# Attention softmax shared between ScalarE and VectorE: VectorE's exponential rebuilt as a sum of four shifted bit patterns, PSUM banks shared, order model remeasured

## The chip, the cores and the metric

The kernel runs on one core of a Trainium2 chip. The metric is the device time of one execution in microseconds (us). Five engines matter: TensorE (PE, with its weight loads PEld), VectorE (DVE), ScalarE (ACT), GpSimd (POOL) and SyncE (SP, which here only issues transfers). TensorE's clock is granted by a throttle, and the trace records it: 1.00 is full speed, 0.50 is half.

On one core a run counts as *slow* when it is more than 1.5% above the fastest run of the same kernel.

## The reference, cut to what matters

```python
# x: [1, 2048, 640], bf16; 32 heads of 20 for the queries, ONE head of keys and values
def reference(...):
    xn = layernorm(x)
    return x + A(xn) + B(xn)

def A(x):                                   # attention, all heads share k and v
    q = (x @ wq) -> [heads, 2048, 20];  k = x @ wk;  v = x @ wv
    p = softmax(q k^T * 20**-0.5)           # 32 x 2048 x 2048 exponentials
    return (p v) @ wo

def B(x):                                   # feed-forward, inner width 1536
    return relu(x @ w1 + b1)**2 @ w2 + b2
```

Most of the time goes to the 134 million exponentials of the softmax.

## The kernel before

The scores are cut into 2,048 tiles of 128 keys x 512 queries: 32 blocks (8 groups of four heads x 4 query chunks), 16 key tiles each, 4 heads each. Per tile, TensorE computes K x Q into one PSUM bank, an engine computes exp from PSUM into SBUF, and TensorE multiplies the result with V. "QK" is the first product and "PV" the second. Four heads run side by side on TensorE: QK tiles the array by rows (contraction over 20 values), and PV and everything else tiles it by columns.

Two engines make exponentials. ScalarE does it directly, on three banks or on two at a time, in alternation:

```python
ACT_BANKS = ((0, 1, 2), (3, 4))     # ScalarE's two sides: 3 banks, then 2
DBANKS = (5,)                       # VectorE's one bank
PVB = 6                             # PV sums
MB = 7                              # projections, FFN, output, one at a time
...
Op(f"ACT{j}", "ACT", 0.064 + 0.4267 * n, [activation(out=PT[:, s0:s0+n, :], in_=ps[:, b0:b0+n, :], func=Exp, ...)])
```

VectorE does it in *sets* of four tiles (four heads of one key tile), by writing an integer into the bit pattern of a bf16 number. `L = x*XA + XB` as a 16-bit integer, read as bf16, is a power of two with a linear mantissa. That is a rough exp. The kernel corrects it with two more terms, made from the same bits:

```python
# four evictions from PSUM, one per tile
d1 = tensor_scalar(out=L[:, cs] as uint16, in0=ps[:, bank, :], scalar1=XA, scalar2=XB, mult, add)      # 0.686
# once per set, on 128 x 2048
W  = tensor_scalar(L, 0xFF80, 124,    bitwise_and, bitwise_or)      # 0.74, the power of two
U  = tensor_scalar(L, 0x7F,   0x3F80, bitwise_and, bitwise_or)      # 0.74, the mantissa
T  = tensor_tensor(L, U, mult)                                      # 1.235
T  = tensor_tensor(T, U, mult)      # VectorE 1.235, in every second set GpSimd in two halves of 2.15
# TensorE adds up: L @ vx  +  W @ (0.5*vx)  +  T @ (CC*vx)           three weighted sums per set
```

The order of all instructions is fixed when the program is built. A greedy list scheduler in Python gives every operation a modelled duration (the numbers in the margins) and a modelled latency between engines. At each step it takes the operation that can start first. VectorE takes a set whenever it has room, and ScalarE gets the other tiles. So *the model decides how many tiles each engine gets*. Where the model sees TensorE less than `FILL` busy during a wait, the scheduler inserts *fillers*: matmuls with zero weights into the PV bank that change nothing and only keep TensorE running:

```python
FILL = 0.7
...
lat = 0.2 if the producer is PE else 0.06                  # latency model
...
while pick[0] > free["PE"] + 0.1 + ... and pe_credit(free["PE"]) < 0.0:      # modelled PE use below FILL
    commit(Op("fill", "PE", 0.215, [mm(ps[...PVB...], zeros32, kT[:, 0:512], False, False, ...) for jj in range(4)]))
```

The softmax here doesn't subtract the row's maximum and nothing guards it: scores larger than these inputs give would overflow.

## Time and profile before

Three runs: 837.78, 837.86 and 1253.41 us. Nothing was recorded that explains the third.

| before, one profiled execution | value |
|---|---|
| span | 840.8 us, mean granted clock 0.962 |
| first exponential starts / last ends | 31.8 / 831.9 us |
| tiles on ScalarE / VectorE | 1,696 / 352 (88 sets) |
| exponential activations | 679 (339 of three banks, 339 of two, 1 rest) |
| filler groups of four matmuls | 272 |

The first fence is cut from the page of the kernel before. It shows the engines' busy times, two rows of busy tenths (40 equal slices of 21 us; PEclk is the granted clock in tenths), the chain that ended last by engine, and then groups of instructions. A group's line gives the source line, engine, operation, output<-input with shapes and count, then busy us and the mean ns of one, then the engine's idle time just before these instructions and what ended it.

```profile
PE 775.6 (92%) x10439; PEld 254.9 (30%) x10439; DVE 678.5 (81%) x973; ACT 794.5 (94%) x724; POOL 268.4 (32%) x168
...
ACT  7589999997989999999999999999899999999995
...
PEclk8689999987989999999999999999999999999999
...
ACT 61%; PE 28%; DVE 6%; issue 1%; DVEq 0%
...
L862 ACT ACTIVATE PT<-ps 128x1536 bf16<-128x1536 f32 (+1 forms) x679 | 775.0, 1294 | 29.3 <-PE ps L549 27.5
...
L978 DVE TENSOR_SCALAR x_sb<-ps 128x512 uint16<-128x512 f32 x352 | 241.3, 685 | 113.2 <-PE ps L549 110.7
...
L989 DVE TENSOR_TENSOR tbuf<-x_sb,ubuf 128x2048 bf16<-128x2048 bf16 x88 | 113.4, 1289 | 0.6
...
L549 PE MATMUL ps<-kT,zeros 128*32 128x512 bf16 x1088 | 87.9, 401 | 0.0
...
L985 DVE TENSOR_SCALAR x_sb<-x_sb 128x2048 uint16<-128x2048 uint16 x88 | 68.6, 780 | 0.5
L987 DVE TENSOR_SCALAR ubuf<-x_sb 128x2048 uint16<-128x2048 uint16 x88 | 66.4, 755 | 0.0
L996 DVE TENSOR_TENSOR tbuf<-tbuf,ubuf 128x2048 bf16<-128x2048 bf16 x44 | 55.5, 1261 | 0.0
```

ScalarE is the bound: 775.0 us of exponentials, and only 29.3 us idle before them, of which 4.3 come before the first one. VectorE's four set operations (the last four DVE lines) cost 304 us against 241 us for the evictions. The line with `kT,zeros` is the fillers: 272 groups of four.

The PEclk row has two dents, at the start and around slices 8 to 11, counted from zero. This is the window view of the kernel before for the second dent. Its columns are window, us, then the busy us of PE, PEld, DVE, ACT and POOL with their counts, granted clock, DMA share and GB/s.

```profile
180.00:200.00 20.00, 19.04 (x150) 4.35 (x153) 11.01 (x18) 14.67 (x13) 5.68 (x3) 0.58 0.01 2
```

With the clock at 0.58, ScalarE was busy only 14.67 of 20 us although TensorE was busy 19.04. It waits there for a TensorE at half speed.

### The profile page before, as it was taken

The numbers are of one execution on the slowest core, as the hardware profiler recorded it, in microseconds if no ns is written. First come the engines' busy times: TensorE is split into PE (matmuls) and PEld (weight loads), VectorE is DVE, ScalarE is ACT, GpSimd is POOL, SyncE is SP. The second block draws the span as 40 slices with busy tenths as digits, with TensorE's granted clock in tenths as the row PEclk, the third lists the DMA queues.
The fourth block names the chain that finished last, engine by engine and source line by source line (L and its number), as shares of the span: only waits on it lengthen the run. The fifth ranks groups of instructions, "written<-read, shape, count | busy, mean of one in ns | idle before, by whom it ended". The sixth has DMA issues, their size and how long they took to land.

```text
span 840.8 us, 22953 instructions
## 1 busy us (share of the span) xinstructions
PE 775.6 (92%) x10439; PEld 254.9 (30%) x10439; DVE 678.5 (81%) x973; ACT 794.5 (94%) x724; POOL 268.4 (32%) x168
## 2 busy tenths in 40 slices
PE   7799999999999999899999999999899999999996
PEld 3232222222223333222223333322222333323332
DVE  5768888776878888889887877889888888888874
ACT  7589999997989999999999999999899999999995
POOL 4424344531222321254432223135343232223221
PEclk8689999987989999999999999999999999999999
DMA  9500000000000000000000000000000000000000
GB/s 306 120 2 2 1 2 2 2 2 1 2 2 17 3 17 18 17 2 2 2 2 2 17 18 17 3 16 2 2 2 2 18 17 18 17 2 2 3 2 33
DMA packets 11714, 14.94 MB, mean 18 GB/s; under 512 B 2017, under 2 KB 10978, under 8 KB 11618
## 3 DMA queue, kind: packets, MB, share of 16 engines
q1 hardware_dynamic: 10306, 13.44, 5.2%
q8 instruction: 81, 1.33, 0.7%
q10 hardware_dynamic: 1312, 0.05, 0.1%
q14 instruction: 15, 0.12, 0.0%
HBM read 10.87 MB, written 2.62 MB: 16 GB/s over the span
## 4 chain that ended last, share of the span: by engine, by line
ACT 61%; PE 28%; DVE 6%; issue 1%; DVEq 0%
ACT PT L862 61%; PE ps L549 28%; DVE x_sb L978 2%; DVE tbuf L989 1%; DVE T L914 1%; DVE ubuf L987 1%; DVE x_sb L985 0%; DVE hT_tmp L668 0%; PE ps L597 0%; DVE out_sb L1171 0%; DVE Tn L912 0%; DVE qT L651 0%; DVE kT L611 0%; DVE OTn L918 0%; PE ps L624 0%
## 5 line engine op out<-in xcount | busy, mean ns | idle before, releaser
L862 ACT ACTIVATE PT<-ps 128x1536 bf16<-128x1536 f32 (+1 forms) x679 | 775.0, 1294 | 29.3 <-PE ps L549 27.5
L549 PE MATMUL ps<-qT,kT 20*128 20x512 bf16 x2048 | 309.7, 393 | 46.3 <-ACT PT L862 33.1
L994 POOL TENSOR_TENSOR tbuf<-tbuf,ubuf 128x1024 bf16<-128x1024 bf16 x88 | 191.6, 2197 | 448.5 <-DVE tbuf L989 448.5
L978 DVE TENSOR_SCALAR x_sb<-ps 128x512 uint16<-128x512 f32 x352 | 241.3, 685 | 113.2 <-PE ps L549 110.7
L549 PE MATMUL ps<-PT,vx 128*32 128x512 bf16 x1696 | 171.1, 397 | 3.3 <-DVE Tn L912 3.1
L549 PEld LDWEIGHTS ps<-qT,kT 20*128 20x128 bf16 x2048 | 75.2, 91 | 313.6 <-ACT PT L862 234.3
L989 DVE TENSOR_TENSOR tbuf<-x_sb,ubuf 128x2048 bf16<-128x2048 bf16 x88 | 113.4, 1289 | 0.6
L549 PE MATMUL ps<-kT,zeros 128*32 128x512 bf16 x1088 | 87.9, 401 | 0.0
L677 POOL TENSOR_TENSOR big<-hT_tmp 128x512 bf16<-128x512 bf16 x48 | 58.1, 1216 | 90.2 <-DVE hT_tmp L668 90.1
L549 PEld LDWEIGHTS ps<-PT,vx 128*32 128x32 bf16 x1696 | 43.3, 93 | 108.4 <-issue 99.1
L549 PE MATMUL ps<-xnT,w_sb 128*32 128x512 bf16 x960 | 72.1, 381 | 1.6 <-DVE hT_tmp L668 1.0
L549 PE MATMUL ps<-w_sb,big 128*32 128x320 bf16 x1536 | 72.8, 301 | 0.8 <-DVE qT L651 0.4
L985 DVE TENSOR_SCALAR x_sb<-x_sb 128x2048 uint16<-128x2048 uint16 x88 | 68.6, 780 | 0.5
L987 DVE TENSOR_SCALAR ubuf<-x_sb 128x2048 uint16<-128x2048 uint16 x88 | 66.4, 755 | 0.0
L996 DVE TENSOR_TENSOR tbuf<-tbuf,ubuf 128x2048 bf16<-128x2048 bf16 x44 | 55.5, 1261 | 0.0
L549 PE MATMUL ps<-wo_pad,OTn 128*32 128x320 bf16 x1024 | 51.2, 300 | 0.7 <-DVE OTn L918 0.7
L549 PE MATMUL ps<-xnT,wq_sb 128*20 128x512 bf16 x620 | 47.4, 388 | 0.2 <-DVE out_sb L731 0.2
L549 PEld LDWEIGHTS ps<-w_sb,big 128*32 128x32 bf16 x1536 | 36.8, 96 | 26.4 <-issue 11.6
L668 DVE TENSOR_SCALAR hT_tmp<-ps,b1col 128x512 bf16<-128x512 f32 x48 | 35.7, 743 | 7.5 <-PE ps L549 7.2
L549 PE MATMUL ps<-x_sb,vx 128*32 128x512 bf16 x352 | 35.8, 397 | 0.8 <-DVE Tn L912 0.8
L549 PE MATMUL ps<-x_sb,vxh 128*32 128x512 bf16 x352 | 35.4, 393 | 0.0
L549 PE MATMUL ps<-tbuf,vxc 128*32 128x512 bf16 x352 | 35.2, 390 | 0.1
(84 smaller groups left out, 363.5 us busy)
## 6 DMA issues: line engine op xcount, KB each, us to landing
w_sb<-in_B_w_dram SPq DMA_DIRECT2D x2, 1920.0 KB, 10.7
xr<-in_A_x_dram SPq DMA_DIRECT2D x16, 160.0 KB, 2.4
out_dram<-out_sb SPq DMA_DIRECT2D x16, 160.0 KB, 1.8
x_sb<-in_A_x_dram SPq DMA_DIRECT2D x3, 640.0 KB, 7.6
wq_sb<-in_A_wq_dram SPq DMA_DIRECT2D x1, 800.0 KB, 10.5
wo_pad<-in_A_wo_dram SPq DMA_DIRECT2D x4, 200.0 KB
x_sb<-in_A_x_dram SPq DMA_DIRECT2D x2, 320.0 KB, 3.7
wk_c<-in_A_wk_dram ACTq DMA_DIRECT2D x1, 25.0 KB, 3.4
```

Source lines behind the costliest of these rows:

```text
L549: return lambda e: e.matmul(out_, l, r, start=start, stop=stop, tile_position=tp)
L668: o = Op(f"RL{qc}_{f}", "DVE", 0.75, [lambda e: e.tensor_scalar(out=hT_tmp[:, k % 2, :], in0=ps[:, MB, :], scalar1=b1col[:, f:f + 1], scal ...
L677: q = Op(f"SQ{qc}_{f}", "POOL", 1.15, [lambda e: e.tensor_tensor(out=h2T[:, qc % 2, f, :], in0=hT_tmp[:, k % 2, :], in1=hT_tmp[:, k % 2, : ...
L862: return Op(f"ACT{st_['j']}", "ACT", 0.064 + 0.4267 * n, [lambda e: e.activation(out=PT[:, s0:s0 + n, :], in_=ps[:, b0:b0 + n, :], func=AF ...
L914: tm = Op(f"TM{b}", "DVE", 0.69, [lambda e: e.tensor_tensor(out=T2[:, a, :].rearrange("p (c d) -> p c d", d=32), in0=Tn[:, a, :].rearrange ...
L978: d1 = dv(f"D1_{n}_{i}", 0.686, lambda e: e.tensor_scalar(out=lbuf[:, a, cs].bitcast(U16), in0=ps[:, bank, :], scalar1=XA, scalar2=XB, op0 ...
L985: s["wop"] = [dv(f"W{n}", 0.74, lambda e: e.tensor_scalar(out=W.bitcast(U16), in0=L.bitcast(U16), scalar1=0xFF80, scalar2=124, op0=ALU.bit ...
L987: s["uop"] = dv(f"U{n}", 0.74, lambda e: e.tensor_scalar(out=ubuf[:, a, :].bitcast(U16), in0=L.bitcast(U16), scalar1=0x7F, scalar2=0x3F80, ...
L989: s["t1"] = [dv(f"T1_{n}", 1.235, lambda e: e.tensor_tensor(out=T, in0=L, in1=ubuf[:, a, :], op=ALU.mult), [s["uop"]] + ([("pv", old, 2)] ...
L994: s["t2"].append(dv(f"T2_{n}", 2.15, lambda e, ks=ks: e.tensor_tensor(out=T[:, ks], in0=T[:, ks], in1=ubuf[:, a, ks], op=ALU.mult), s["t1" ...
L996: s["t2"].append(dv(f"T2_{n}", 1.235, lambda e: e.tensor_tensor(out=T, in0=T, in1=ubuf[:, a, :], op=ALU.mult), s["t1"], 4))
```

## The change

The intent is to take tiles away from ScalarE. Four parts belong together:

1. **VectorE's formula.** exp is now a weighted sum of the *same* rough pattern shifted by quarters of an octave, `L`, `L+32`, `L+64` and `L+96`. A shift is one integer add. Half of the adds go to GpSimd. TensorE pays with four weighted sums per set instead of three.
2. **PSUM.** ScalarE gets two sides of two banks. The three banks 4, 5 and 7 are shared by VectorE's tiles and by the projections, FFN and output.
3. **The order model.** Latencies and durations were measured again, and most VectorE operations got shorter. ScalarE's sides are planned when their banks come free.
4. **GpSimd.** Its integer add is written as add *and multiply by 1.0*. The squarings of the FFN move to VectorE.

The diff, cut to its core:

```diff
-CC = 0.1640625
+NTERM = 4
+TSTEP = 128 // NTERM
+TW = [1.0, 0.83984375, 0.70703125, 0.59375]
-ACT_BANKS = ((0, 1, 2), (3, 4))
-DBANKS = (5,)
+ACT_SIDES = ((0, 1), (2, 3))
+SHARED = (4, 5, 7)
-SWITCH = 0.1
+NSET = 3
+SWITCH = 0.105
+PASS = (("DVE", "POOL", "POOL"), ("DVE", "POOL", "DVE"))
+LATS = {("PE", "ACT"): 0.215, ("PE", "DVE"): 0.215, ("ACT", "PE"): 0.21, ("DVE", "PE"): 0.145, ("DVE", "DVE"): 0.0, ...}
...
-            t = max(t, d.fin + d.lat)
+            t = max(t, d.fin + (d.lat if d.lat is not None else LATS.get((d.eng, self.eng), 0.1)))
...
-            d1 = dv(f"D1_{n}_{i}", 0.686, ...
-            s["wop"] = [dv(f"W{n}", 0.74, ... bitwise_and, bitwise_or
-            s["uop"] = dv(f"U{n}", 0.74, ... bitwise_and, bitwise_or
-            s["t1"] = [dv(f"T1_{n}", 1.235, ... tensor_tensor mult
-            ... second multiply, VectorE or GpSimd
+            d1 = dv(f"D1_{n}_{i}", 0.60, ...
+            for j in range(1, NTERM):
+                eng = PASS[n % len(PASS)][j - 1]
+                p = dv(f"P{j}_{n}", 0.60 if eng == "DVE" else 1.9,
+                       tensor_scalar(out=T as uint16, in0=L as uint16, scalar1=TSTEP * j, scalar2=1.0 if POOL else None,
+                                     op0=ALU.add, op1=ALU.mult if POOL), ..., eng)
...
+            bank = min(fb, key=bank_state)          # whichever shared bank is free first
...
-                q = Op(f"SQ{qc}_{f}", "POOL", 1.15, ...
+                q = Op(f"SQ{qc}_{f}", "DVE", 0.34, ...
```

The built program has 120 sets where it had 88, and 1,568 tiles on ScalarE where it had 1,696, in 784 activations of two banks. It has 1,552 switches between row and column tiling where it had 1,352. It has 19 filler groups where it had 272.

## The prediction

> **What bounds it now.** ScalarE. The engine table gives ACT 794.5 of 840.8 us (94%); the chain that ended last is 61% the PSUM-to-PT exponential and 28% matmuls. The exponential starts at 31.8 us and ends at 831.9 (timeline). It runs as 339 activations of three banks and 339 of two; alternating chains advance 1.137 us per activation (38.58 us for 34 in the merged chain), i.e. 0.427 us per 512-column tile plus about 0.07 fixed. 1,696 tiles x 0.427 + 679 x 0.07 = 771 us; only 29.3 us are idle before that line. So the wall is ACT work plus about 70 us of start, tail and gaps.
>
> **What the change does (counts from the built order).** VectorE now makes 120 sets of four tiles instead of 88, so ACT keeps 1,568 tiles, in 784 activations of exactly two banks: 1,568 x 0.427 + 784 x 0.07 = 724 us, 47 us less. That is the gain, nearly all of it on the chain. The two-bank grouping alone costs ACT about 7 us against the old mix.
>
> VectorE per set: four evictions stay (685 ns each, 0.60 apart back to back), but mask, mask, multiply and the shared second multiply (0.69 + 0.69 + 1.22 + 0.6) become on average 1.5 integer adds (685 ns class). The squarings come over from GpSimd (48 x about 0.35). My estimate for DVE busy: 480 x 0.61 + 180 x 0.62 + rest about 175 = 580 us against 678.5. GpSimd: 180 passes; from 529 ns at 128 elements and 904 at 640 I estimate 1.9 us at 2,048, so POOL busy about 365 us. The Trainium skill, "SBUF — State Buffer", section "Who interferes with whom", says a GpSimd op and a two-port VectorE op exclude each other for a whole instruction. This trace agrees: the same 685 ns mask was once 2,410 ns. I expect some adds stretched, but DVE has room.
>
> TensorE: four weighted sums per set instead of three (480 quads for 264), more mode switches between row and column tiling (1,552 for 1,352, about 0.11 us each in the timeline), fills down from 272 quads to 19. Real work: 789 row groups and 1,296 quads x 0.215, 672 x 0.136, switches: about 710 us at full clock, before about 620 plus 58 of fills. PE is now almost level with ACT: 0.91 of 0.92 us per step, with 0.28 us of slack for the refill of a two-bank side. Here part of the gain is lost: I allow 20 us of ACT waiting for PE. The granted clock also dips to about half (0.58 in 180 to 200 us, where ACT lost 5 us); I allow 15 us for such dips and 9 for the start.
>
> **Sum.** 724 + 20 + 15 + 9 = 768 us of exponential phase, plus 31.8 before and 9 after, minus 3 for span against timed run: **805 us**, range **788 to 823**. Chances: faster by over 2% 0.85, within 2% 0.12, slower 0.03.
>
> **What would show it.** Right: exponential activations 784, group sum near 724 us net of overlap; ACT idle before them 40 to 60 us, ended by PE; a chain with more matmul share than before (over 35%); DVE busy near 580; POOL near 365 with passes near 1.9 us. Wrong: passes on GpSimd well over 2 us, or VectorE adds often stretched beyond 1.5 us, with TensorE waiting on evictions; or long half-clock stretches.
>
> **What would make it wrong.** Upwards: PE saturation, since a static order with both engines full turns every dip of the clock into time; slow GpSimd passes. Downwards: a denser TensorE may never drop its clock, giving about 790.

## The result, and the profile after

Four runs: 798.87 (clock 0.937, slow, and the one that was profiled), 776.55 (0.971), 783.14 (0.963) and 774.64 us (0.974). Ratios here and below are those of the record, from fast runs alone, this kernel over the kernel before; they are not quite the ratios of the medians that I quote. The ratio is 0.930 (95% interval 0.923 to 0.937). I ran the same kernel again six times (run e1): 775.0, 776.0 and 775.0 at clock 0.976 to 0.978, and 794.6, 794.6 and 840.0. The fast time is about **775 us**, 30 us below the predicted 805 and below the range.

Lines of the page of the kernel after, from the slow execution of 797.1 us. They answer to the lines of before:

```profile
PE 778.4 (98%) x10163; PEld 230.2 (29%) x10163; DVE 623.4 (78%) x1019; ACT 744.6 (93%) x830; POOL 361.3 (45%) x215
...
PEclk8659999998655899999999999999999999999999
...
ACT 79%; PE 17%; DVE 0%; issue 0%; DVEq 0%
...
L908 ACT ACTIVATE PT<-ps 128x1024 bf16<-128x1024 f32 x784 | 724.9, 1189 | 33.7 <-PE ps L564 33.3
...
L1044 POOL TENSOR_SCALAR tmore<-x_sb 128x2048 uint16<-128x2048 uint16 x60 | 113.3, 1897 | 142.2 <-DVE tmore L1044 86.7
...
L1044 DVE TENSOR_SCALAR tmore<-x_sb 128x2048 uint16<-128x2048 uint16 x60 | 47.3, 800 | 0.5
```

The same page of the same kernel in a fast execution (e1, 773.3 us):

```profile
PE 752.4 (97%) x10163; PEld 228.0 (29%) x10163; DVE 624.6 (81%) x1020; ACT 741.2 (96%) x831; POOL 360.0 (47%) x213
...
PEclk8759999999999999999999999999999999999999
...
L908 ACT ACTIVATE PT<-ps 128x1024 bf16<-128x1024 f32 x784 | 720.6, 1203 | 13.2 <-PE ps L564 13.0
```

The exponential's group fell from 775.0 to 720.6 us. Its idle time fell from 29.3 to 13.2 us in the fast execution and rose to 33.7 in the slow one. The two executions of one program differ by one dent in the PEclk row. The chain of waits says the same. Here it is in the slow execution (start, us, what, count), cut to the long pieces:

```profile
60.87 133.94 ACT PT L908 x146
...
194.85 17.06 PE ps L564 x108
211.91 10.19 ACT PT L908 x11
...
222.15 45.02 PE ps L564 x322
267.17 484.27 ACT PT L908 x528
```

And in the fast one (e1):

```profile
58.20 669.40 ACT PT L908 x730
```

In the fast execution 730 activations follow each other without a break, in 669.40 us, or 0.917 us each. In the slow one TensorE takes over the chain from 194.85 to 267.17, with one interlude. The window view of the slow execution shows what happens there:

```profile
160.00:180.00 20.00, 19.92 (x251) 5.22 (x247) 18.57 (x33) 20.00 (x23) 10.82 (x6) 1.00 0.01 2
...
190.00:192.00 2.00, 1.69 (x24) 0.31 (x14) 1.68 (x3) 2.00 (x4) 1.65 (x1) 1.00 0.00 0
192.00:194.00 2.00, 1.55 (x22) 0.50 (x22) 2.00 (x5) 2.00 (x4) 0.01 (x1) 1.00 0.00 0
...
196.00:198.00 2.00, 2.00 (x16) 0.32 (x8) 2.00 (x3) 1.19 (x2) 1.75 (x1) 0.50 0.00 0
...
240.00:260.00 20.00, 20.00 (x162) 3.99 (x162) 10.13 (x16) 12.75 (x14) 5.66 (x3) 0.50 0.00 1
```

At full clock (160 to 180) TensorE is full and ScalarE is busy all 20.00 us, with 23 activations. At 190 to 194 TensorE has a thin stretch (1.69 and 1.55 of 2 us). At 196 the clock is 0.50, and until 267, except from 212 to 222, TensorE is busy at half speed: from 240 to 260 it is busy 20.00 of 20 us while ScalarE makes 14 activations instead of 23.

Where the 67.5 us between the two profiled spans went (840.8 before, 773.3 after in e1):

| part of the span | before | after (e1) | difference |
|---|---|---|---|
| until the first exponential | 31.8 | 31.9 | +0.1 |
| exponential work | 775.0 | 720.6 | -54.4 |
| ScalarE idle between exponentials (the group's idle less the wait before the first: 29.3 - 4.3, 13.2 - 5.1) | 25.0 | 8.1 | -16.9 |
| after the last exponential | 8.9 | 12.7 | +3.8 |

The profiled execution of before was not one of its best: its fast runs in the later batches have medians of 833 to 836, and its span of 840.8 answers to a time of about 842.5. So, by estimate from those medians, some 6 to 10 of these 67.5 us belong to that one execution, whose clock was 0.962 where runs of 832 us show 0.98; between typical fast runs the change is worth about 58 to 61 us.

### The profile page after: what moved, and what is told of

Its sections match the earlier page's. It is cut to its first block, busy times and chain, and to the rows that moved or that the text cites. A ratio compares the mean times of both kernels' runs of the same rounds, so it can differ in the third digit from the quotient of the medians.

```text
span 797.1 us, 22583 instructions
## 1 busy us (share of the span) xinstructions
PE 778.4 (98%) x10163; PEld 230.2 (29%) x10163; DVE 623.4 (78%) x1019; ACT 744.6 (93%) x830; POOL 361.3 (45%) x215
## 4 chain that ended last, share of the span: by engine, by line
ACT 79%; PE 17%; DVE 0%; issue 0%; DVEq 0%
ACT PT L908 79%; PE ps L564 16%; PE ps L624 0%; DVE out_sb L1243 0%; PE ps L652 0%; DVE xnT L348 0%; DVEq L135 0%; DVE vx L391 0%; DVE kT L389 0%; PE ps L669 0%
## 5 line engine op out<-in xcount | busy, mean ns | idle before, releaser
L908 ACT ACTIVATE PT<-ps 128x1024 bf16<-128x1024 f32 x784 | 724.9, 1189 | 33.7 <-PE ps L564 33.3
L1035 DVE TENSOR_SCALAR x_sb<-ps 128x512 uint16<-128x512 f32 x320 | 212.0, 683 | 62.5 <-PE ps L564 60.6
L1044 POOL TENSOR_SCALAR tmore<-x_sb 128x2048 uint16<-128x2048 uint16 x60 | 113.3, 1897 | 142.2 <-DVE tmore L1044 86.7
L1044 POOL TENSOR_SCALAR x_sb<-x_sb 128x2048 uint16<-128x2048 uint16 x60 | 113.2, 1897 | 127.5 <-DVE x_sb L1044 51.2
L1044 POOL TENSOR_SCALAR tmore<-tmore 128x2048 uint16<-128x2048 uint16 x60 | 113.3, 1897 | 120.5 <-DVE tmore L1044 67.2
L1035 DVE TENSOR_SCALAR tmore<-ps 128x512 uint16<-128x512 f32 x160 | 105.8, 683 | 24.7 <-PE ps L564 23.4
L564 PE MATMUL ps<-tmore,vxs 128*32 128x512 bf16 x960 | 86.6, 396 | 0.0
L1044 DVE TENSOR_SCALAR tmore<-x_sb 128x2048 uint16<-128x2048 uint16 x60 | 47.3, 800 | 0.5
L564 PE MATMUL ps<-x_sb,vxs 128*32 128x512 bf16 x480 | 45.1, 397 | 0.0
L1044 DVE TENSOR_SCALAR tmore<-tmore 128x2048 uint16<-128x2048 uint16 x60 | 44.5, 753 | 0.3
```

The lines of the kernel that those rows point to most:

```text
L564: return lambda e: e.matmul(out_, l, r, start=start, stop=stop, tile_position=tp)
L908: return Op(f"ACT{st_['j']}", "ACT", 0.05 + 0.4267 * n, [lambda e: e.activation(out=PT[:, s0:s0 + n, :], in_=ps[:, b0:b0 + n, :], func=AF. ...
L1035: d1 = dv(f"D1_{n}_{i}", 0.60, lambda e: e.tensor_scalar(out=L[:, cs].bitcast(U16), in0=ps[:, bank, :], scalar1=XA, scalar2=XB, op0=ALU.mu ...
L1044: p = dv(f"P{j}_{n}", 0.60 if eng == "DVE" else 1.9, lambda e, T=T, j=j, two=(eng == "POOL"): e.tensor_scalar(out=T.bitcast(U16), in0=L.bi ...
```

## The experiments

My theory after the result was this. The gain is ScalarE's smaller load, as predicted. The waits of ScalarE for TensorE, which I had added to it, do not exist at full clock, because the shared banks and the new order hide them (which of the two does it, no run here isolates). What remains is the clock. The rivals were that the remeasured model made the gain by itself (R1), that GpSimd's adds made it (R2), and that the formula alone, at equal load, already beats the old one (R3). All kernels gave correct results. "Early" below means two edits to the start of the program, given at e9.

### e1: the kernel after, again

No edit. It was meant to get a profile of a fast run, which is shown above.

> The changed kernel again, for a profile in the fast state and the spread. Theory A (ScalarE sets the time and never waits for TensorE while its clock is full): the 784 exponentials advance 0.917 us each in every stretch at full clock, ACT idle before them is 10 to 15 us in a fast run and nearly all of it lies in the start, before 61 us; time 774 to 784. Theory B (TensorE at its limit costs about 20 us of waits, as the prediction allowed): 20 us or more of ACT idle spread over full-clock stretches.

Measured: median 785.3 over fast and slow runs together, fast runs 775.0 to 776.0, ratio 0.930 (0.925 to 0.935). All 13.2 us of idle lie before 58.2 us. At the start TensorE is at half clock, as this window of e1 shows:

```profile
40.00:60.00 20.00, 20.00 (x170) 5.17 (x171) 7.31 (x14) 14.15 (x15) 7.25 (x6) 0.56 0.00 1
```

So at full clock ScalarE waits for nothing in this order.

### e2: VectorE held to the old 88 sets

```diff
+CAP = 88
+            if n >= CAP / NBLK * progress() + 2 or n >= CAP:      # in new_set()
+                return None
```

> VectorE held to 88 sets as before the change, spread evenly; everything else of the change kept, so 848 two-bank activations instead of 784. Theory A: 64 x 0.917 = 59 us more than the changed kernel, about 835 us, so all of the gain is the larger share of VectorE. Rival C (the new order model and the shared banks bring a good part of the gain by closing gaps): well below, 815 us or less.

Measured: 951.5, 972.7, 1019.0 and 1063.9 us at clocks 0.815 to 0.707. That is slower than before, and far beyond any expectation. The clock row of the profiled execution shows about a third of its slices at half speed. These are that row and then the windows of one warm and one cold stretch of e2:

```profile
PEclk8555569999999999998899555555557975699997
```

```profile
260.00:280.00 20.00, 19.67 (x260) 5.87 (x260) 10.54 (x16) 20.00 (x23) 7.55 (x4) 1.00 0.01 2
660.00:680.00 20.00, 20.00 (x144) 3.44 (x142) 8.16 (x14) 13.26 (x14) 5.66 (x3) 0.50 0.00 1
```

In the warm stretch ScalarE runs 23 activations per 20 us with no idle time, just as with 120 sets. In the cold one it runs 14. The share of tiles could not be read from this run, because the clock covers it. e7 does nearly the same with more fillers (243 groups instead of the 121 of e2), so that the clock holds.

### e3: the kernel after with the old model

```diff
-LATS = {("PE", "ACT"): 0.215, ...}
+LATS = 0.2 from PE, 0.06 from any other engine
-SWITCH = 0.105;  D1 0.60;  adds 0.60;  RL 0.66;  QT 0.60;  TN 0.63;  RC 0.155;  ...
+SWITCH = 0.1;    D1 0.686; adds 0.74;  RL 0.75;  QT 0.66;  TN 0.72;  RC 0.25;   ...
```

> The changed kernel with the latencies and durations of the old order model (0.06 and 0.2 us flat, VectorE evictions 0.686, and so on); still 120 sets and 784 activations, but another order. Theory A with an order that hardly matters: within 1% of the changed kernel. Rival C: the remeasured numbers are what lets both engines run full; then ACT idle before the exponentials grows to over 30 us and the time by 15 us or more.

Measured: fast runs 807.7 (clock 0.939) and 797.3 (0.954), slow ones 831.5 and 841.2, ratio 0.962 (0.954 to 0.971). It has the same 120 sets and 784 activations. The windows of a stretch at full clock, first e3 and then e1:

```profile
260.00:400.00 140.00, 140.00 (x2002) 43.25 (x1999) 115.24 (x185) 139.94 (x152) 67.12 (x36) 1.00 0.04 11
```

```profile
260.00:400.00 140.00, 139.58 (x1925) 41.18 (x1921) 120.03 (x190) 140.00 (x155) 70.11 (x38) 1.00 0.04 11
```

With the old model three activations fewer fit into 140 us, which is 2%. The rest of the loss comes from more time at half clock: a start that stays cold until about 90 us, and dips at 417 to 421 and 718 to 745. Part of that can be chance: the order of the start differed from build to build (see e6). So theory A's "within 1%" failed, and the model matters for this kernel by at least those 2%, through the order and not through the share of tiles.

### e4: GpSimd's add as a single operation

```diff
-two=(eng == "POOL")
+two=False
```

> The GpSimd adds as one operation instead of add and multiply by one; same order, same values. If the form matters, a pass takes clearly longer than the 1.90 us of the changed kernel (my guess 2.5 us or more), VectorE adds stretch over 2 us more often, and the time grows by over 10 us. If it does not, 1.90 us and no change of time.

Measured: 1320.0 to 1331.6 us, ratio 1.588, clock 0.56 to 0.585. The view of the adds' source line (duration in ns as min/median/max, first and last start), first in e4:

```profile
L1044 POOL TENSOR_SCALAR x_sb<-x_sb x60: 5362/5363/5793, 39.3 to 1268.7; 128x2048 uint16<-128x2048 uint16 x60
L1044 DVE TENSOR_SCALAR tmore<-x_sb x60: 652/694/5840, 48.1 to 1276.4; 128x2048 uint16<-128x2048 uint16 x60
```

And in e1:

```profile
L1044 POOL TENSOR_SCALAR x_sb<-x_sb x60: 1899/1900/1902, 40.7 to 732.9; 128x2048 uint16<-128x2048 uint16 x60
L1044 DVE TENSOR_SCALAR tmore<-x_sb x60: 652/687/2207, 48.4 to 738.1; 128x2048 uint16<-128x2048 uint16 x60
```

The same add costs GpSimd 5,363 ns as one operation and 1,900 ns with a multiplication by 1.0 behind it. VectorE's slowest add grew with it, from 2,207 to 5,840 ns: each time about the length of one GpSimd pass. The Trainium skill, "SBUF — State Buffer", section "Who interferes with whom", says that between GpSimd and a VectorE operation in a two-port mode, the one that issues first holds the shared port pair for a whole instruction while the other is blocked. Both maxima agree: the excess over the median is 1,520 and 5,146 ns, each under one pass of 1,900 and 5,363 ns. GpSimd is busy for only 986 of the 1,330 us, and ScalarE's 496.5 us of idle time lie almost all at half clock; how the long passes lead there was not isolated.

### e5: keeping TensorE busy in the gap before the first exponentials

In e1 there is a gap of 5.21 us ahead of the first QK. These are lines of e1's timeline (start, us, engine, line, what, and in brackets the idle time before and what ended it), cut to the gap:

```profile
24.54 5.88 DVE L324 TENSOR_SCALAR big<-x_sb,rstd,nmr 128x640 bf16<-128x640 bf16 x3
25.15 4.37 POOL L412 MEMSET wo_pad<- 128x5120 bf16 x1
25.63 0.44 PE L338 MATMUL ps<-ident,big 128*128 128x128 bf16 x5
31.29 1.04 PE L564 MATMUL ps<-qT,kT 20*128 20x512 bf16 x6 [5.21 <-DVE vx L391]
```

Three VectorE normalizations, elsewhere 0.43 to 0.93 us each, took 5.88 us. One of them alone took 5.15 us: it stood still beside a GpSimd fill (a memset) of 4.37 us. TensorE had nothing to do, and its clock fell. e5 fills the gap:

```diff
         em_wo_late()
+        pe_dummies(22)
```

> The changed kernel with 22 extra full-array matmuls into an unused bank put before the main loop, where TensorE idled 5.2 us (26.1 to 31.3 us) and its clock then stood at half until 57.5. Theory D (a few microseconds of low TensorE activity halve the clock, and a busy stretch keeps it): the clock stays near 1.0 from 31 to 58 us, the 13 us of ACT idle there shrink below 6, and the fast runs fall from 775 to 765 to 769. Rival E (the dip belongs to the row-tiled work itself or to the chip, not to the gap): clock still about 0.5 there, time unchanged or 1 us longer. The dip near 200 us should come as often as before.

Measured: 773.9 to 775.1 in four runs (clock 0.981 to 0.982), 782.3 and 782.4 in two (0.968), ratio 0.929. I had expected several us of gain, and there is none. The local effect is there, as this window shows where e1 had 0.56:

```profile
40.00:44.00 4.00, 4.00 (x53) 1.01 (x49) 2.78 (x5) 4.00 (x6) 1.88 (x2) 1.00 0.01 4
```

But the profiled execution (774.7 us) has a dip at 207 to 231 that the profiled e1 does not have. ScalarE idles 7.3 us in it, and 7.7 us at half clock in the start of e1: there, the gain of the start was paid back. The other five runs were not profiled.

### e6: more fillers in the kernel after

```diff
-FILL = 0.7
+FILL = 0.9
```

> The changed kernel with the filler threshold at 0.9 instead of 0.7: 52 groups of zero-weight matmuls instead of 19, put where the order leaves gaps. Theory D: the dip near 180 to 270 us, that made runs of 795 to 840 us, becomes rare: most runs within 5 us of 775, median about 777. Rival E: the spread of the runs stays, with a median of 785 or more.

Measured: five runs of 762.2 to 763.5 at clock 0.995 and one slow (781.0), ratio 0.912 (0.908 to 0.916). It has 52 filler groups instead of 19. This build also drew a better start: exponentials begin at 27.7 us instead of 31.9. The order of the program's first 30 us comes from a loop over a Python set, and it differs from build to build. So e6 alone does not say how much the fillers did; e9 and e10 do.

### e7: 88 sets with the clock held

```diff
+CAP = 88        # as e2; 89 sets came out, 846 activations
-FILL = 0.7
+FILL = 0.9
```

> VectorE held to 88 or 89 sets as in the earlier run at 996 us, now with the filler threshold at 0.9 (243 groups instead of 121). Theory A with D: the clock holds, ACT is again the limit with 846 activations at 0.917, so 62 x 0.917 = 57 us over 775, about 832 (start dip perhaps longer: up to 850). Rival E: the half clock comes regardless of fillers, 900 us or more.

Measured: 818.1 (clock 0.993), 827.2 (0.979), and 833.3 and 836.1 (slow), ratio 0.984 (0.975 to 0.992). With the load of the old kernel, the new formula, banks, model and fillers together are worth 1.6% (0.8 to 2.5). R3 falls as the main cause: the formula pays because VectorE can make more sets with it.

### e8: the kernel before without fillers

```diff
-FILL = 0.7
+FILL = 0.0
```

> The kernel before without its 272 groups of fillers. Theory D: TensorE falls to half clock for long stretches, 900 us or more, so the fillers were what kept the kernel before at speed. Rival E: the time stays near 832, or falls a little as TensorE has less to do.

Measured: 879.6 to 888.6, clock 0.838 to 0.854, ratio 1.058. The 272 filler groups were worth about 49 us (medians of this batch: 885.3 and 836.1) to the kernel before, or more, since this build also drew an earlier start (26.8 us instead of 31.8). That is less than I had expected.

### e9: the kernel after with a fixed and earlier start ("early")

```diff
-            unsched = set(tasks.keys())
+            unsched = dict.fromkeys(tasks)              # the order no longer differs between builds
...
+        add(P.pool, lambda e: e.memset(wo_pad[:], 0.0), inc=c_pool)      # at the head of GpSimd's queue
...
-            add(P.pool, lambda e: e.memset(wo_pad[:], 0.0), waits=[], inc=c_pool)
```

> In every build so far the prologue's order differed, since its scheduler walks a Python set; in the builds that began late a 4.36 us GpSimd memset of wo_pad held a two-port VectorE operation for 4 to 6 us. Here the prologue has a fixed order and that memset stands at the head of GpSimd's queue; filler threshold still 0.7. Expected: no VectorE operation of over 2 us before the first exponential, which then begins at about 27 us instead of 31; TensorE's gap before it under 3 us, so the clock mostly stays full and ACT idle falls from 13 to under 6: fast runs 758 to 768. The dip near 200 us still comes in some runs (spread over 10 us).

Measured: 769.1 to 771.4 in four runs, 791.5 and 791.7 in two (clock 0.948), ratio 0.920 (0.914 to 0.926). Exponentials begin at 26.8 us. The 4.37 us fill no longer stands beside a VectorE normalization. The fast runs miss the expected 758 to 768 by a little: ScalarE idles 8.3 us in the profiled one, 7.2 of them at half clock in a dip at 203 to 226.

### e10: e9 with more fillers

```diff
-FILL = 0.7
+FILL = 0.9
```

> The same fixed prologue with the filler threshold at 0.9. If fillers are what removes the dip near 200 us: all runs within 3 us of each other, 757 to 763, mean clock 0.99. If the good run at 762 us was only a lucky prologue: no difference from the run with 0.7 beside it, in median or spread.

Measured: all six runs within 760.9 to 763.6, clock 0.992 to 0.997, ratio 0.911 (0.906 to 0.916). Nothing else differs from e9, and both ran in one batch on one chip. From the pages, the clock row of e9, then the clock row and the exponential's group of e10:

```profile
PEclk8999999999769999999999999999999999999999
```

```profile
PEclk8999999999999999999999999999999999999999
...
L908 ACT ACTIVATE PT<-ps 128x1024 bf16<-128x1024 f32 x784 | 719.0, 1205 | 0.8 <-PE ps L564 0.7
```

The dip is gone, and so is the second group of times. ScalarE is idle for 0.8 us in 719, most of it before the first activation. I looked at every window of 2 us between 60 and 690 us. In e10 none has TensorE busy below 1.75 us. In e1, e5, e9 and the slow execution of the kernel after, four to six have, most of them between 176 and 222 us, and there the dips begin. In e9 this is the pair around its start:

```profile
200.00:202.00 2.00, 1.27 (x16) 0.35 (x16) 2.00 (x2) 2.00 (x4) 1.77 (x1) 1.00 0.00 0
202.00:204.00 2.00, 2.00 (x22) 0.30 (x15) 1.74 (x4) 2.00 (x3) 1.01 (x1) 0.62 0.00 0
```

e1 has such windows too (1.48 us at 192, 1.10 us at 214) and kept its clock. A thin stretch makes a dip possible, not certain. The Trainium skill, "TensorE: Matmul & The Clock Gate", section "What's actually happening", describes a gate that watches a free-running window of activity and passes half of the pulses after an idle one. The runs agree so far: the same order dips in one execution and not in the next. The traces show more. In all 17 of them, every stretch at one clock between the first change and the last is a whole multiple of 3.41 us (the dip of e9 is 23.89 us, the cold start of e1 27.31). I cut each trace into windows of that grid and took TensorE's busy share from 35 us on. The clock fell 64 times, each time at the end of a window with a share of at most 0.85, and 49 of these were below 0.75; of the 3,244 windows that kept full clock, 16 were below 0.75. The slow execution shows 0.73 and 0.74 (191.4 to 194.8 and 218.7 to 222.1) in the windows before its two dips. In e1 the grid lies elsewhere and cuts its thin stretches into windows of 0.81, 0.90 and 0.79, and the clock stays. So whether a dip comes depends on how a thin stretch falls on the grid. This is read from traces; no run moves the grid, and between 0.63 and 0.85 both outcomes occur. e10 is the best version I ran, and it beats both kernels: 761.65 us, median of six.

### e11: e10 with two shared banks instead of three

```diff
-SHARED = (4, 5, 7)
+SHARED = (5, 7)
```

> As the run before, but bank 4 taken out of the shared pool (two shared banks, 5 and 7, instead of three). The order then finds room for only 95 sets, 834 activations: 50 x 0.917 = 46 us more than with three banks, about 806, with ACT still busy throughout. If banks do not matter beyond that count, no further loss.

Measured: 803.6 to 804.3 at clock 0.994 to 0.998, ratio 0.961. With two banks the order holds only 95 sets, so ScalarE has 834 activations. From its page:

```profile
L908 ACT ACTIVATE PT<-ps 128x1024 bf16<-128x1024 f32 x834 | 765.3, 1180 | 0.9 <-PE ps L564 0.8
```

Compared with e10, ScalarE has 46.3 us more work and practically the same idle time. The program takes 42.2 us longer; 4.1 us came back in a shorter tail (9.7 us after the last exponential instead of 13.8) and 0.6 in an earlier start. The clock was full in both, with 207 filler groups here and 52 in e10. This is the cleanest test of the theory: time follows ScalarE's load, and the third bank is what lets VectorE carry 25 of the sets.

### e12: the kernel before with the new model

```diff
 before.py
+LATS = {...}                                    # as in the kernel after
-SWITCH = 0.1;   D1 0.686; W, U 0.74; T 1.235; ...
+SWITCH = 0.105; D1 0.60;  W, U 0.60; T 1.13;  ...
+                                                # and the start of e9
```

> The kernel before with only the remeasured durations and latencies in its order model (and the fixed prologue), formula and banks as before: 91 sets, 674 activations instead of 679. ACT work falls by about 6 us. If the order model alone closes the gaps of the kernel before: idle before the exponentials falls from 29 to about 10 us and the time to 805 to 815. If not: 820 to 832.

Measured: 852.8, 855.8 and 860.8 (clock 0.942 to 0.956), 867.1 slow, ratio 1.023 (1.015 to 1.032). I had expected a gain. The model gives VectorE only three more sets (91), and from the page the exponential's group now waits more:

```profile
L866 ACT ACTIVATE PT<-ps 128x1536 bf16<-128x1536 f32 (+1 forms) x674 | 773.4, 1265 | 42.3 <-PE ps L553 39.8
```

Why this order is worse I did not settle. The trace points to the clock: 25.8 of the 42.3 us of idle time lie at half clock (12.6 of 29.3 in the kernel before), and the order has 220 filler groups where it had 272. The new model with more fillers was not run on the kernel before. But R1 falls all the same: the exponentials alone take 773.4 us here, and with the start (26.8) and the tail (9.0) that is 809 us even if ScalarE never idled, well above 775.

### e13: the kernel before with the start of e9

The edit is that of e9, on the kernel before.

> The kernel before with the fixed prologue and the early memset of e9, nothing else. Its fast runs at 832 contain the same late start and half-clock start: if so, 832 falls by 8 to 15 us, to 817 to 824, and the pair with the same prologue (e9 at 769.5) differs by 48 to 55 us, the 52 us of ACT work (771 to 719) that left. If the start is no part of it, 830 to 834.

Measured: 824.5 to 832.6, median 829.25, ratio 0.9935 (0.9885 to 0.9985). I expected more. It gained 4 to 5 us (medians 832.84 and 829.25, ratio 0.9935) although exponentials begin 3.3 us earlier and are idle 19.9 us instead of 29.3 in the profiled execution. The median of the kernel before that I compare with was a few us better than its profiled execution. With equal starts the change is worth about 60 us: e13 829.25, e9 769.5 (medians of fast runs, from two batches). That is above the 48 to 55 that I had expected; 53.3 us of it are exponential work (774.0 and 720.7).

### e14: e13 with more fillers

```diff
-FILL = 0.7
+FILL = 0.9
```

> The same with the filler threshold at 0.9: 585 groups of fillers instead of 272. The kernel before loses little to clock dips after the start, so at best 3 us less than e13; more likely the fillers get in the way of real matmuls, since its order model is not exact, and it is up to 10 us slower than e13. Either way over 805, 45 us or more above e10.

Measured: 846.0 and 847.1 (clock 0.992), 855.2 and 855.7 (0.980), ratio 1.021 (1.014 to 1.029). It holds the clock and is still slower by about 22 us than e13, where I had allowed 10. In the kernel before, the model sees so many gaps that 585 filler groups go in, where 272 were. TensorE's busy time rises from 767.3 to 816.6 us (97% of the span), and VectorE gets 87 sets. That fillers stand in front of real work there is my reading; no run isolates it. It fits that 24.8 of ScalarE's 25.1 us of idle time lie at full clock, where e13 has 10.8. In the kernel after, the same setting adds only 33 groups.

### e15: e10 with all adds on VectorE

```diff
-PASS = (("DVE", "POOL", "POOL"), ("DVE", "POOL", "DVE"))
+PASS = (("DVE", "DVE", "DVE"),)
```

> As e10, but all three adds of a set on VectorE, none on GpSimd: 119 sets and 786 activations. VectorE gets about 90 adds of 0.6 us more, 54 us, and no longer waits for GpSimd's lock: DVE busy 650 to 690. Since ACT is the limit and VectorE has room, 762 to 766, as e10. If VectorE's load matters, evictions come late, TensorE and ACT wait, and it is over 775.

Measured: 762.9 to 763.8 at clock 0.994 to 0.998, ratio 0.914, against 0.911 for e10 in another batch. From its page:

```profile
PE 748.0 (98%) x10291; PEld 231.6 (30%) x10291; DVE 685.5 (90%) x1193; ACT 742.0 (97%) x833; POOL 20.4 (3%) x33
```

GpSimd is busy for 20.4 us instead of 360, VectorE for 685.5 us instead of 620, and there are still 119 sets. R2 falls. The adds on GpSimd, two-operation form included, carry none of the gain. (The squarings of the FFN stay on VectorE here; moving them alone was not tested.)

### All runs in one table

| run | fast runs, us | clock of these | ratio | sets |
|---|---|---|---|---|
| after, first comparison | 774.6, 776.6, 783.1 | 0.963-0.974 | 0.930 | 120 |
| e1 same | 775.0-776.0 | 0.976-0.978 | 0.930 | 120 |
| e2 88 sets | 951.5 | 0.815 | - | 88 |
| e3 old model | 797.3, 807.7 | 0.939-0.954 | 0.962 | 120 |
| e4 single-operation add | 1320-1332 | 0.56-0.59 | 1.588 | 120 |
| e5 busy gap | 773.9-782.4 | 0.968-0.982 | 0.929 | 120 |
| e6 more fillers | 762.2-763.5 | 0.995 | 0.912 | 120 |
| e7 88 sets, more fillers | 818.1, 827.2 | 0.979-0.993 | 0.984 | 89 |
| e8 before, no fillers | 879.6-888.6 | 0.838-0.854 | 1.058 | 88 |
| e9 early | 769.1-771.4 | 0.978-0.982 | 0.920 | 120 |
| e10 early, more fillers | 760.9-763.6 | 0.992-0.997 | 0.911 | 120 |
| e11 two shared banks | 803.6-804.3 | 0.994-0.998 | 0.961 | 95 |
| e12 before, new model | 852.8-860.8 | 0.942-0.956 | 1.023 | 91 |
| e13 before, early | 824.5-832.6 | 0.975-0.988 | 0.994 | 88 |
| e14 before, early, more fillers | 846.0-855.7 | 0.980-0.992 | 1.021 | 87 |
| e15 all adds on VectorE | 762.9-763.8 | 0.994-0.998 | 0.914 | 119 |

## Why the prediction was wrong

It had the direction and the mechanism right and was 30 us too high. The fast time lies below its range. Set against e1, term by term:

| term of the sum | predicted | measured (e1) |
|---|---|---|
| until the first exponential | 31.8 | 31.9 |
| exponential work | 724 | 720.6 |
| ScalarE idle between exponentials: waiting for TensorE at full clock | 20 | 0 |
| the same: dips of the clock after the start | 15 | 0 |
| the same: the start | 9 | 8.1 (all before 58.2 us, while the clock was low) |
| after the last exponential | 9 | 12.7 |
| timed run less span | -3 | +1.7 |
| sum | 805 (805.8 unrounded) | 775 |

**The step that failed is "Here part of the gain is lost: I allow 20 us of ACT waiting for PE", together with the 15 us for dips.** The number behind the first was about right: I had 0.91 of 0.92 us per step for TensorE, and it was 97% busy. What I drew from it was wrong. Two engines that are both nearly full need not wait for each other when the order keeps the next side ready. At full clock ScalarE waited for nothing: 730 activations in 669.40 us, and 0.8 us of idle time in the whole of e10. Presumably the slack for the refill of a side (I had computed 0.28 us) was enough; no run varies it alone. e3 shows that this depends on the order: with the old model, 2% fewer activations fit at full clock.

**The dips were charged as an average over states.** The ten runs of this kernel are five of 774.6 to 776.6 (e1's profile, one of them, has no dip in the middle), one of 783.1, three of 794.6 to 798.9 and one of 840.0. Against the first five the others lost some 8, 20 or 65 us at lower clocks (0.963, 0.937 to 0.946, 0.884), and my 15 us is true of none of them. I named "a denser TensorE may never drop its clock" as the way to be wrong downwards and gave 790 for it, still with the 20 us of waits inside. That does happen, but because of fillers and not of density alone: e9, at 98% busy, still dips in its profiled fast run, and e10, also at 98%, does not.

**ScalarE's load was right.** 784 activations, predicted 724 us and measured 720.6. I had 2 x 0.427 + 0.07 = 0.924 us for a step, and the chain shows 0.917. e11 confirms that the time follows this load, since 50 activations more cost 42.2 us.

**VectorE was undersized.** I estimated 580 us and it was 624.6 in e1. Two terms make the difference. The adds took 759 to 811 ns in the mean where I had 620 (138.3 us instead of 112); their median is 687, and the rest is stretching, up to 2.2 us, beside GpSimd, which I had expected in kind. And the 480 evictions took 317.6 us where I had 293. It cost nothing, since e15 carries 685.5 us without losing time.

**GpSimd was right.** I said 365 us and 1.9 us a pass; it was 360.0 us and 1.900. It was also of no use to the time (e15).

**The chain was read the wrong way round.** I had said that the share of matmuls in the chain would rise above 35%. It fell to 17% in the slow execution and 9% in the fast one. I had also predicted 40 to 60 us of idle time before exponentials, and they were 13.2 (33.7 in the slow one).

**The timed run is longer than the span, not shorter.** I had subtracted 3 us because the profiled execution of before was 840.8 us long while the median was 837.86. These were different executions. For one and the same execution the time is 1.7 us above the span (e1: 775.03 and 773.3).

What stays open is this. What exactly the throttle counts, and why the clock stays low for so long once it has fallen; the traces show only the grid and TensorE's busy share before a fall. How much of the rest each part of the change carries: the formula, the two-bank sides, the planning of these sides and the moved squarings were never tested alone. Why the kernel before gets worse with the new model (e12). And the one run of 1253 us.

## What to carry to other kernels

When the engine that bounds a kernel is relieved, cost the relief, and do not add a wait only because the next engine is nearly full: look for that wait in the trace, at full clock, before charging for it. Keep the clock's states apart in a prediction, one number for each, because their mean need not be near any run. And where TensorE's clock falls after thin stretches, fillers in just those stretches can pay: 33 more groups of four brought about 8 us and removed the whole second state here (e10), and 272 were worth about 49 us to the kernel before (e8). Their number alone does not decide: 313 more on top of these lost 22 us (e14), while e11 carries 207 with 0.9 us of idle time. Measure it for each order.

## What the Trainium skill lacked or had wrong

- "TensorE: Matmul & The Clock Gate", section "What's actually happening", says that the clock comes back after one busy window of about 3.4 us and falls after an idle one. Here it stayed at 0.50 through 44 us (222 to 267 in the slow execution of the kernel after) and through 205 us (537 to 742 in e2), while the trace, in which the ends of matmuls are modelled, shows TensorE busy for at least 19.80 of every 20 us from 540 to 740 in e2. It fell after windows of 3.41 us that were still 66 to 83% busy in the runs of the kernel after, e2, e3, e5 and e9 (0.73 and 0.74 in the slow execution, 0.70 in e9), and after one of 79% it once did not (e1). The page does not say what share of a window counts as busy.
- "GPSIMD Engine Reference", section 4.1, says that GpSimd runs elementwise operations with one input at roughly line rate. A 128x2048 uint16 add with an immediate took 5,363 ns as one operation and 1,900 ns as add-and-multiply (e4, e1), and VectorE took 687 ns for it. The section does not tell the two forms apart.
- "SBUF — State Buffer", section "Who interferes with whom", has the general rule for GpSimd and a two-port VectorE operation, but it names no GpSimd memset, which only writes. Here a VectorE normalization with one tensor input took 5.15 us beside a memset of 4.37 us, where others take 0.43 to 0.93 (e1); with the memset moved to the head of the queue none took over 0.93 us (e9).
